# One fused attention and mixture-of-experts kernel: the packing stage's loads, score buffers and weight conversion rearranged

## Chip, cores and metric

The kernel runs on one core of one Trainium2 chip. The metric is device microseconds (us) of one execution; three runs of the kernel before gave a median of 1285.65 us (1284.27 to 1286.92). The core has five engines that run side by side and wait for one another by semaphores: TensorE (PE), VectorE (DVE), ScalarE (ACT), GpSimd (POOL) and SyncE (SP), which here issues nearly all DMAs.

## What is computed

The reference, cut to what matters (8 batches, 8 heads, 576 positions of 64; 32 packing queries; 4608 tokens of 512):

```
p_packed = sm_attn(p, k, v)              # 32 packing queries per head over 576 keys
out      = sm_attn(q, p_packed, p_packed)
x = transpose(out) to (4608, 512)
h = x @ w_in;  g = 0 below -1, (h+1)^2/4 between, h above 1;  x = g @ w_out     # d_ff 2048
expert = argmax(x @ w_gate) of 8
out[mask] = gate * (relu(x[mask] @ w1[e]) @ w2[e])                              # per expert
```

The dense weights arrive as float64 bit patterns (two 32-bit words an element) and are turned into float32 on the chip, each split into a high and a low part, since every float32 product is made of three matmuls in a shorter format (high by high, high by low, low by high).

## The kernel before

**Packing stage.** For each of 16 groups `i` (8 batches, two groups of four heads each) the kernel loads K (`kp`, 576 KB, L372) and V (`vr`, 512 and 64 KB, L376 and L377), forms the scores `sc` on PE (L385), takes their maximum on DVE (L392), exponentiates on ACT (L395), transposes the result on PE (`tp`, `av`, L403 and L405), copies it out of PSUM on ACT (L406 to L408) and multiplies it by V (`av`, L418). `build_pk` (L169) then turns the packed rows into operands (`bt`, L173, read out by ACT and DVE, L182 to L184). K and V have three places each, `kp0` to `kp2` and three for `vr`, so the loads for group i + 3 go where group i was. `sc` has one buffer of two PSUM banks (L351).

**Weights beside it.** 16 units of dense weights, 1 MB each (`wr`, L264), are converted one half at a time by `prep_half` (L267): one ACT pass (L282), four DVE passes on integers and floats (L283 to L286), a cast to the high part on ACT (L287) and the low part on DVE (L288), all 128 x 512. Units 0 and 1 of every four are first-layer weights: they go to a staging place (`ws0`, `ws1`), are multiplied by the packed operands (`first_product`, `pp`, L326; its result `pw`, L329 and L330), and are written back to DRAM by `spill` (L304) for the later batches. The other two are second-layer weights and stay (`wo`). NU = 9 units are converted in the packing loop (L459), spread evenly over its 16 turns; the other seven follow one in each of the first steps of the dense layer (L1009). The raw data of a unit shares three places (`RAW`, L254), so the load of unit u + 3 is issued behind the conversion of unit u.

**Dense layer.** 12 token tiles in 16 steps each. A step makes 128 hidden columns (`h`, `ffn1`, L698), applies the nonlinearity on ACT and DVE (`hidden`, L715 to L731), and adds the previous step's part to the output (`tile_y`, three or four PSUM banks `y`, L703 to L705). Three of the 16 steps of tile 0 are written inside the packing loop (L467). PE, ACT, DVE and POOL instructions are put in order by a list scheduler, so pieces of step 0 and later steps stand among the packing's instructions; SP keeps the order in which the program is written. Behind the dense layer come routing and the expert slots.

The PSUM has eight banks. Before, `y` has three, which `bt` and the second scores `s` (L211) share in the packing stage (L166); `h` one, `a` two, `sc` two. After packing the two banks of `sc` become `late` (L1013).

Of the kernel before, what the change touches and what calls it, by code (L numbers as in the profile page):

```python
# [8 lines left out]
F32 = mybir.dt.float32  # L9
# [28 lines left out]
NU = 9  # L38
# [53 lines left out]
def attn_moe_kernel(ctx, tc, qT, kT, vv, pT, wcat, wg, w2cat, out):  # L92
# [15 lines left out]
    wsd = dram.tile([2 * NQ, 2, P, 2, 512], F32, name="wsd")  # L108
# [12 lines left out]
    pool.memset(half, 0.5)  # L121

# [70 lines left out]
    def attn_chain(col0, b, ws, n, g, ah, al, pl, sfx):  # L193
# [73 lines left out]
    def prep_half(u, i):  # L267

        raw = wraw[u][:, i]
        n, m = divmod(u, 4)  # L270
        if m < 2:
            w = wtile(f"ws{m}{i}", [P, 2, 512], F32R, f"ws{u}_{i}")
            wstage[2 * n + m, i] = w
        else:
            if i == 0:
                wout[2 * n + m - 2] = wtile(f"wo{2 * n + m - 2}", [P, 2, 2, 512], F32R, f"wo{u}")
            w = wout[2 * n + m - 2][:, i]
        hi, lo = w[:, 0, :], w[:, 1, :]
        low, high = raw[:, :, 0], raw[:, :, 1]
        ca = s1.tile([P, 512], I32, name=f"ca{u}_{i}", tag="ca", bufs=4)  # L280
# [9 lines left out]
    loaded = [0]  # L290

    def more_units(n):
        while loaded[0] < n:
            load_unit(loaded[0])
            loaded[0] += 1

    def after_unit(u, n):
        if u and (u - 1) % 4 < 2:
            spill((u - 1) // 4, (u - 1) % 4)
        more_units(min(u + 4, n))  # L300

    def spill(n, g):
        for q in range(2):
            sp.dma_start(wsd[2 * n + g, q], f32(wstage[2 * n + g, q]))  # L304

    def reload(p, n, k):
        w = wtile(f"ws1{k % 2}", [P, 2, 512], F32R, f"ws{p}_{n}_{k}")
        sp.dma_start(f32(w), wsd[2 * n + k // 2, k % 2])
        wstage[2 * n + k // 2, k % 2] = w
# [6 lines left out]
    def first_product(n, g):  # L316
# [4 lines left out]
        for par in range(2):  # L321
            ps = a_tile([P, 512], f"pp0_{n}_{g}_{par}")
            i = 0
            for q in range(2):
                for t, m in ((0, 0), (0, 1), (1, 0)):
                    pe.matmul(ps, lhsT=one(2 * g + q, t, par), rhs=wstage[2 * n + g, q][:, m, :], start=(i == 0), stop=(i == 5))  # L326
                    i += 1
# [4 lines left out]
    def product(p, n, k):  # L332
# [5 lines left out]
        for i, (t, m) in enumerate(((0, 0), (0, 1), (1, 0))):  # L338
            pe.matmul(ps, lhsT=both(k, t), rhs=wstage[2 * n + g, q][:, m, :], start=(i == 0), stop=(i == 2))
# [756 lines left out]
```

## Time and profile before

| | us |
|---|---|
| median of three runs | 1285.65 |
| the profiled execution, its own time | 1285.13 |
| its span, first to last instruction | 1283.1 |

The profile is of that one execution. Beside the busy time of each engine it gives the share of the 16 DMA engines' time, the DMA rate, and the clock that TensorE was granted. A row of the timeline is: start, duration, engine, line, operation, result and operand, shapes, count, and in brackets how long the engine stood idle before and what released it.

### The profile page before, as it was taken

The page shows a single profiled execution, that of the slowest core. Times are in us where ns is not written, and L with a number is a line of the kernel's source. Part 1 is how long each engine was busy: PE and PEld are TensorE (multiplying, and loading weights), DVE is VectorE, ACT ScalarE, POOL GpSimd, SP SyncE. Part 2 cuts the span into 40 slices and gives each one's busy share as a digit, 9 for nine tenths or more (in the row PEclk, how much of TensorE's full clock was granted, in tenths as well). Part 3 has the DMA queues.
Part 4 walks back from the last instruction along what each step waited for, and adds up shares of the span by engine and source line. Part 5 has one row for each costly group of instructions (what it writes and reads, how often), then busy time and mean ns, then how long its engine had stood idle before and what let it go on. Part 6 is the DMA issues. An engine that isn't in the chain of part 4 may idle for free. (4 is left out here: it accounts for less than half of the span.)

```text
span 1283.1 us, 22131 instructions
## 1 busy us (share of the span) xinstructions
PE 1206.7 (94%) x7234; PEld 999.4 (78%) x7234; DVE 947.2 (74%) x2440; ACT 755.5 (59%) x1733; POOL 422.2 (33%) x682
## 2 busy tenths in 40 slices
PE   3778999999999999999999998998999999999997
PEld 2446778788778887678888876776899999999996
DVE  6766996988885959978769598688566665666653
ACT  4646666667665567566565555644556556566563
POOL 3220014723841205741112266767312112121120
PEclk9889999999999999999999999899999999999999
DMA  8967782044111232111331104201521211112150
GB/s 297 322 241 255 268 255 83 34 142 159 44 36 50 74 125 86 51 41 37 124 105 38 44 9 161 62 1 51 164 75 34 67 34 55 46 42 59 34 173 21
DMA packets 71339, 128.26 MB, mean 100 GB/s; under 512 B 10409, under 2 KB 46761, under 8 KB 69040
## 3 DMA queue, kind: packets, MB, share of 16 engines
q1 hardware_dynamic: 56528, 96.28, 22.9%
q0 software_dynamic: 5840, 18.95, 3.9%
q10 hardware_dynamic: 8848, 11.54, 2.9%
q8 instruction: 60, 0.98, 0.3%
q14 instruction: 63, 0.52, 0.1%
HBM read 162.31 MB, written 31.77 MB: 151 GB/s over the span
## 5 line engine op out<-in xcount | busy, mean ns | idle before, releaser
L698 PE MATMUL h<-ah,pw 128*128 128x256 f32 (+1 forms) x1024 | 243.1, 302 | 15.4 <-DVE rt L717 14.3
L868 PEld LDWEIGHTS gh<-gx,sw 128*128 128x128 f32 x1728 | 231.4, 193 | 14.2
L506 DVE CUSTOM_DVE_ANT_0 jk<-yr,wgb 128x512 bf16<-128x512 f32 x288 | 232.0, 806 | 9.9 <-ACT yr L756 7.9
L868 PE MATMUL gh<-gx,sw 128*128 128x256 f32 x1728 | 235.4, 285 | 0.0
L703 PE MATMUL y<-wo,gh 128*128 128x512 f32 x576 | 231.4, 402 | 2.1 <-ACT gh L730 1.2
L704 PE MATMUL y<-wo,gh 128*128 128x512 f32 x576 | 228.6, 397 | 0.0
L852 DVE TENSOR_TENSOR sw<-raw,sw 128x512 fp32r<-128x512 f32 x264 | 169.5, 693 | 74.9 <-ACT sw L851 74.9
L698 PEld LDWEIGHTS h<-ah,pw 128*128 128x128 f32 x1024 | 175.8, 189 | 40.9 <-DVE rt L717 23.3
L851 ACT CAST sw<-raw 128x512 fp32r<-128x512 f32 x304 | 169.2, 617 | 59.7 <-PE gy L705 55.4
L705 PE MATMUL y<-wo,gl 128*128 128x512 f32 x576 | 187.9, 399 | 1.6 <-POOL gl L731 1.2
L715 ACT ACTIVATE rt<-h,half 128x320 f32<-128x320 f32 (+1 forms) x192 | 111.2, 580 | 110.1 <-PE h L698 69.6
L698 PE MATMUL h<-al,pw 128*128 128x256 f32 (+1 forms) x512 | 152.4, 298 | 0.4 <-POOL al L232 0.4
L730 ACT CAST gh<-rt 128x256 fp32r<-128x256 f32 (+2 forms) x256 | 100.6, 417 | 80.1 <-DVE rt L717 57.8
L717 DVE SCALAR_TENSOR_TENSOR rt<-h,rt 128x320 f32<-128x320 f32 (+1 forms) x192 | 105.5, 550 | 51.4 <-ACT rt L716 49.7
L703 PEld LDWEIGHTS y<-wo,gh 128*128 128x128 f32 x576 | 108.8, 189 | 26.9 <-ACT gh L730 4.7
L705 PEld LDWEIGHTS y<-wo,gl 128*128 128x128 f32 x576 | 105.7, 189 | 29.0 <-POOL gl L731 2.9
L704 PEld LDWEIGHTS y<-wo,gh 128*128 128x128 f32 x576 | 109.1, 189 | 18.5
L836 POOL TENSOR_TENSOR gx<-xT,gx 128x1024 fp32r<-128x1024 f32 (+1 forms) x19 | 45.1, 2376 | 235.6 <-ACT gx L835 220.4
L704 PE MATMUL gy<-sw,ggh 128*128 128x512 f32 x288 | 115.0, 399 | 0.0
L703 PE MATMUL gy<-sw,ggh 128*128 128x512 f32 x288 | 114.7, 398 | 0.0
L872 ACT ACTIVATE ggh<-gh 128x256 fp32r<-128x256 f32 x144 | 55.0, 382 | 98.4 <-PE gh L868 93.8
L731 DVE TENSOR_TENSOR gl<-rt,gh 128x64 fp32r<-128x64 f32 (+1 forms) x192 | 92.4, 497 | 23.0 <-ACT gh L730 15.2
(221 smaller groups left out, 1874.9 us busy)
## 6 DMA issues: line engine op xcount, KB each, us to landing
raw<-in_w2cat SPq DMA_DIRECT2D x76, 1024.0 KB
ws<-wsd SPq DMA_DIRECT2D x48, 512.0 KB
wr<-in_wcat SPq DMA_DIRECT2D x16, 1024.0 KB
kp<-in_kT SPq DMA_DIRECT2D x16, 576.0 KB
xb<-xs SPq DMA_DIRECT2D x72, 128.0 KB
vr<-in_vv SPq DMA_DIRECT2D x16, 512.0 KB
wsd<-ws SPq DMA_DIRECT2D x16, 512.0 KB
qr<-in_qT ACTq DMA_DIRECT2D x16, 320.0 KB
```

Of the source, the lines that this page charges most:

```text
L506: dve.tensor_tensor_reduce(out=junk, in0=rows[j][:, :DM], in1=wgb[0][:, e, :], scale=1.0, scalar=0.0, op0=ALU.mult, op1=ALU.add, accum_out ...
L698: pe.matmul(ps[:, col0:col0 + n], lhsT=w[:, g, part, c], rhs=x[:, g, col0:col0 + n], start=(n_mm == 0), stop=(n_mm == 5))
L703: pe.matmul(y, lhsT=gh, rhs=wh, start=first, stop=False)
L704: pe.matmul(y, lhsT=gh, rhs=wl, start=False, stop=False)
L705: pe.matmul(y, lhsT=gl, rhs=wh, start=False, stop=last)
L715: act.activation(v[:, :W], ps[:, :W], AF.Relu, bias=half, scale=0.5)
L717: dve.scalar_tensor_tensor(out=v[:, :W], in0=ps[:, :W], scalar=1.0, in1=v[:, :W], op0=ALU.max, op1=ALU.min)
L730: act.copy(hi, v[:, c0:c1])
L731: lo_eng.tensor_tensor(out=lo, in0=v[:, c0:c1], in1=f32(hi), op=ALU.subtract)
L851: act.copy(w[:, 0, :], r)
L852: lo_engine(sid, i, n).tensor_tensor(out=w[:, 1, :], in0=r, in1=f32(w[:, 0, :]), op=ALU.subtract)
L868: pe.matmul(ps[:, :SL], lhsT=first(sid, 4 * (fc // 4) + k, part)[:, c], rhs=rh[:, k, :], start=(n_mm == 0), stop=(n_mm == 3 * KD - 1))
```

## The change

Groups' loads, units and PSUM banks of the packing stage are rearranged:

- K and V of a group are loaded separately: K of group i + 3 and V of group i + 2 in turn i, and each unit's load two units ahead, behind the V load. At the start, unit 0 stands between K and V of group 0, unit 1 in group 1, unit 2 behind K of group 2 (before: all three units between group 0 and group 1).
- A unit is converted whole: 128 x 1024 passes, one staging place each for `ws0` and `ws1`, one write-back DMA instead of two, sent behind the product that reads the unit. In tile 1 and later, other users of `ws0` and `ws1` (`kept`, `gx`, `reload`) take the joined places.
- NU = 12 units are converted in the packing loop, four behind it. Units 12 to 15 are loaded at the end of the loop's turn 15.
- `sc` has two buffers (four banks). Until they are given back in turn 15, only one bank `y0` serves `bt`, `s` and `y`; then four `late` banks open (`y1`, `y2`, `h`, `a2`), during the last turns instead of behind the loop.
- The loads of `qr` (queries of tile 0) during packing go from the ACT queue to SP. A one-element exponential `warm` stands at the start of ACT.

```diff
-NU = 9
+NU = 12
...
+    warm = const.tile([P, 1], F32, name="warm")
+    act.activation(warm, half, AF.Exp)
...
+    n_y = [0]
+    def y_tile(name):
+        i = n_y[0] % 3 if late else 0
+        n_y[0] = i + 1
+        return (late[0] if i else psm).tile([P, 512], F32, name=name, tag=f"y{i}")
...
-            return psm.tile([P, 512], F32, name=name, tag="y", bufs=3)
+            return y_tile(name)
...
-            act.dma_start(qr[:, :, :n], qT[b, 2 * g:2 * g + 2, :, ws:ws + n].rearrange("q p s -> p q s"))
+            (act if done else sp).dma_start(qr[:, :, :n], qT[b, 2 * g:2 * g + 2, :, ws:ws + n].rearrange("q p s -> p q s"))
...
-    def prep_half(u, i):
+    def prep_unit(u):
...
-        low, high = raw[:, :, 0], raw[:, :, 1]
-        ca = s1.tile([P, 512], I32, name=f"ca{u}_{i}", tag="ca", bufs=4)
+        low, high = raw[:, :, :, 0], raw[:, :, :, 1]
+        ca = s1.tile([P, 2, 512], I32, name=f"ca{u}", tag="ca", bufs=2)
...
     def spill(n, g):
-        for q in range(2):
-            sp.dma_start(wsd[2 * n + g, q], f32(wstage[2 * n + g, q]))
+        sp.dma_start(wsd[2 * n + g], f32(wstage[2 * n + g]))
...
-        with tc.tile_pool(name="st1p", bufs=1, space=PSUM) as p1:
+        p1_cm = tc.tile_pool(name="st1p", bufs=2, space=PSUM)
+        p1 = p1_cm.__enter__()
...
             s1_load(0)
-            more_units(3)
+            load_unit(0)
+            s1_load_v(0)
             s1_load(1)
+            load_unit(1)
+            s1_load_v(1)
             s1_load(2)
+            load_unit(2)
...
+                if i == NG - 1:
+                    p1_cm.__exit__(None, None, None)
+                    late.append(ctx.enter_context(tc.tile_pool(name="late", bufs=1, space=PSUM)))
...
                 if i + 3 < NG:
                     s1_load(i + 3)
-                for u, j in halves[2 * NU * i // 16:2 * NU * (i + 1) // 16]:
-                    prep_half(u, j)
-                    if j == 1:
-                        if u % 4 < 2:
-                            todo.append((u // 4, u % 4))
-                        after_unit(u, 12)
+                if i + 2 < NG:
+                    s1_load_v(i + 2)
+                for u in range(-(-NU * i // NG), min(-(-NU * (i + 1) // NG), NU)):
+                    prep_unit(u)
+                    if 0 < u < NU - 2:
+                        load_unit(u + 2)
+                    if u % 4 < 2:
+                        todo.append((u // 4, u % 4))
                 if i >= 5 and todo and todo[0][0] < 2:
-                    first_product(*todo.pop(0))
+                    first_product(*todo[0])
+                    spill(*todo.pop(0))
+                if i == NG - 1:
+                    for u in range(NU, FC):
+                        load_unit(u)
...
             for n, g in todo:
                 first_product(n, g)
+                spill(n, g)
```

How the change moves instructions is shown at three places. In these rows `kp0` to `kp2` are the places of K, `vr0` is V of group 0, `wr0` the raw data of unit 0, `wsd` the write-back in DRAM; a number behind an underscore only tells buffers apart.

On SP, the first loads of the program, behind the packing queries (before, then the change):

```order
L372 DMA kp0_158<-in_kT 128x2x576
L376 DMA vr0_170<-in_vv 128x4x256
L377 DMA vr0_170<-in_vv 64x256
L264 DMA wr0_175<-in_wcat 128x2048
L264 DMA wr1_177<-in_wcat 128x2048
L264 DMA wr2_179<-in_wcat 128x2048
L372 DMA kp1_160<-in_kT 128x2x576
L376 DMA vr1_184<-in_vv 128x4x256
L377 DMA vr1_184<-in_vv 64x256
L372 DMA kp2_162<-in_kT 128x2x576
L376 DMA vr2_190<-in_vv 128x4x256
L377 DMA vr2_190<-in_vv 64x256
```

```order
L371 DMA kp0_160<-in_kT 128x2x576
L275 DMA wr0_174<-in_wcat 128x2048
L379 DMA vr0_176<-in_vv 128x4x256
L380 DMA vr0_176<-in_vv 64x256
L371 DMA kp1_162<-in_kT 128x2x576
L275 DMA wr1_182<-in_wcat 128x2048
L379 DMA vr1_184<-in_vv 128x4x256
L380 DMA vr1_184<-in_vv 64x256
L371 DMA kp2_164<-in_kT 128x2x576
L275 DMA wr2_190<-in_wcat 128x2048
L439 DMA pc1_167<-in_pT 128x512
L371 DMA kp0_160<-in_kT 128x2x576
```

K of group 1 stood behind three units and now stands behind one; V of group 2 has moved behind the next group's K.

On PE, around the last scores (`sc15`), before and in the change. `h0_4` is step 4 of tile 0, `y0_2` the third output bank of tile 0; x4 counts matmuls:

```order
L698 MATMUL h0_4_1562<-ah0_194,pw0_1_1_852 128x256
L403 MATMUL tp14_1250<-ident_73,kp2_162 128x128 x4
L385 MATMUL sc15_1270<-kp0_158 64x288 x4
L405 MATMUL av13_1200<-ident_73,kp1_160 64x128
L418 MATMUL av13_1200<-vr13_993 32x64 x20
L403 MATMUL tp15_1303<-ident_73,kp0_158 128x128 x4
L405 MATMUL av14_1255<-ident_73,kp2_162 64x128
L703 MATMUL y0_3_1403<-wo2_509,gh0_1346 128x512
```

```order
L714 MATMUL h0_1_1339<-ah0_193,pw0_0_1_593 128x256
L388 MATMUL sc14_1186<-kp2_164 64x288 x4
L719 MATMUL y0_2_1362<-wo2_356,gh0_1306 128x512
L720 MATMUL y0_2_1362<-wo2_356,gh0_1306 128x512
L421 MATMUL av13_1166<-vr13_1059 32x64 x20
L388 MATMUL sc15_1238<-kp0_160 64x288 x4
L721 MATMUL y0_2_1362<-wo2_356,gl0_1307 128x512
L714 MATMUL h0_2_1383<-ah0_193,pw0_0_0_592 128x256
```

Before, `h0_1` to `h0_4` and three banks of two steps of `y` stand ahead of `sc15`; in the change `h0_1` and the first two matmuls of `y0_2` do, and `tp14` has moved behind it.

On SP, from the last K load on (before, then the change):

```order
L372 DMA kp0_158<-in_kT 128x2x576
L376 DMA vr15_1147<-in_vv 128x4x256
L377 DMA vr15_1147<-in_vv 64x256
L304 DMA wsd_72<-ws5_0_932 128x1024
L304 DMA wsd_72<-ws5_1_996 128x1024
L264 DMA wr9_1160<-in_wcat 128x2048
L264 DMA wr10_1268<-in_wcat 128x2048
L264 DMA wr11_1331<-in_wcat 128x2048
L304 DMA wsd_72<-ws8_0_1313 128x1024
L304 DMA wsd_72<-ws8_1_1322 128x1024
L264 DMA wr12_1539<-in_wcat 128x2048
```

```order
L371 DMA kp0_160<-in_kT 128x2x576
L379 DMA vr14_1114<-in_vv 128x4x256
L380 DMA vr14_1114<-in_vv 64x256
L275 DMA wr11_1126<-in_wcat 128x2048
L379 DMA vr15_1174<-in_vv 128x4x256
L380 DMA vr15_1174<-in_vv 64x256
L275 DMA wr12_1285<-in_wcat 128x2048
L275 DMA wr13_1287<-in_wcat 128x2048
L275 DMA wr14_1289<-in_wcat 128x2048
L275 DMA wr15_1291<-in_wcat 128x2048
L299 DMA wsd_72<-ws8_992 128x2048
L299 DMA wsd_72<-ws9_1117 128x2048
```

Unit 11's load moves in among the last groups' loads. Units 12 to 15 now stand directly behind the last V load, and the write-backs of units 8 and 9 (`ws8`, `ws9`) behind all four.

## Rows read from the trace of the kernel before

**Rows 1.** The page: the span, and each engine's busy time.

```profile
span 1283.1 us, 22131 instructions
...
PE 1206.7 (94%) x7234; PEld 999.4 (78%) x7234; DVE 947.2 (74%) x2440; ACT 755.5 (59%) x1733; POOL 422.2 (33%) x682
```

**Rows 2.** Busy time by stretch: length, engines, then clock, DMA share, GB/s.

```profile
0.00:122.00 122.00, 83.23 (x873) 51.38 (x875) 84.83 (x213) 66.52 (x179) 25.39 (x110) 0.93 0.80 276
122.00:136.00 14.00, 12.55 (x136) 9.31 (x137) 6.96 (x16) 8.42 (x20) 0.00 (x0) 1.00 0.97 354
136.00:186.00 50.00, 46.68 (x279) 36.41 (x277) 50.00 (x98) 33.60 (x60) 4.67 (x5) 1.00 0.71 240
...
200.00:1283.10 1083.10, 1050.25 (x5880) 890.46 (x5878) 800.26 (x2103) 640.33 (x1464) 389.01 (x564) 0.99 0.21 68
```

**Rows 3.** Who waited for whom, 0 to 122 us (total, times, longest); then SP's queue.

```profile
PE tp L403 <- ACT kp L395: 14.3, 6, 7.0
...
PE sc L385 <- DMA kp<-in_kT: 10.0, 2, 7.0
...
SPq L376 <- PE av L418: 68.5, 12, 11.2
```

**Rows 4.** SP's timeline: a stop at a V load, and the last K load.

```profile
20.91 0.54 SPq L372 DMA_DIRECT2D kp<-in_kT  x1
32.71 0.37 SPq L376 DMA_DIRECT2D vr<-in_vv  x1
...
114.64 0.58 SPq L372 DMA_DIRECT2D kp<-in_kT  x1
```

**Rows 5.** PE's timeline: scores 1, a step of h and y, and scores 15.

```profile
18.60 1.71 PE L385 MATMUL sc<-kp 128*64 128x288 f32 x6 [1.25 <-DVE ws L288]
...
104.41 0.28 PE L698 MATMUL h<-ah,pw 128*128 128x256 f32 x1
...
105.85 0.39 PE L703 MATMUL y<-wo,gh 128*128 128x512 f32 x1
106.08 0.40 PE L704 MATMUL y<-wo,gh 128*128 128x512 f32 x1
...
121.91 0.95 PE L385 MATMUL sc<-kp 128*64 128x288 f32 x6
```

**Rows 6.** The page's list of DMA issues: count and size of each kind.

```profile
wr<-in_wcat SPq DMA_DIRECT2D x16, 1024.0 KB
kp<-in_kT SPq DMA_DIRECT2D x16, 576.0 KB
...
vr<-in_vv SPq DMA_DIRECT2D x16, 512.0 KB
wsd<-ws SPq DMA_DIRECT2D x16, 512.0 KB
```

**Rows 7.** Busy time in the two stretches in which loads ran without a gap.

```profile
8.00:24.00 16.00, 6.82 (x63) 3.31 (x59) 12.14 (x28) 10.12 (x22) 4.44 (x10) 1.00 1.04 369
40.00:64.00 24.00, 17.30 (x192) 9.74 (x190) 20.51 (x55) 15.54 (x52) 6.16 (x14) 0.86 1.00 357
```

**Rows 8.** DVE's timeline: passes of 128 x 512, one directly behind the other.

```profile
142.02 0.42 DVE L284 TENSOR_SCALAR ca<-ca 128x512 int32<-128x512 int32 x1
142.35 0.68 DVE L286 SCALAR_TENSOR_TENSOR ca<-wr,ca 128x512 int32<-128x512 int32 x1
142.95 0.69 DVE L731 TENSOR_TENSOR gl<-rt,gh 128x512 fp32r<-128x512 f32 x1
```

**Rows 9.** DVE groups by shape: the same operation at 512 and at 256 columns.

```profile
L731 DVE TENSOR_TENSOR gl<-rt,gh 128x512 fp32r<-128x512 f32 x64 | 45.3, 708 | 12.2 <-ACT gh L730 10.9 <-PE pp L339 0.7 <-ACT ah L231 0.3
...
L731 DVE TENSOR_TENSOR gl<-rt,gh 128x256 fp32r<-128x256 f32 x64 | 27.6, 431 | 0.4
```

**Rows 10.** PE and ACT timelines: the first `bt` and the last copy that reads it.

```profile
16.65 0.48 PE L173 MATMUL bt<-ident,packed 128*64 128x128 f32 x2 [0.71 <-ACT packed L419]
...
28.38 0.18 ACT L184 COPY pkf<-bt 64x32 f32<-64x32 f32 x1
```

More of the change, by code (lines that the diff above doesn't have):

```diff
@@ L288, in prep_half @@
         dve.tensor_tensor(out=lo, in0=f32(ca), in1=f32(hi), op=ALU.subtract)
[L290 to L300, printed above, removed]
     def spill(n, g):
-        for q in range(2):
-            sp.dma_start(wsd[2 * n + g, q], f32(wstage[2 * n + g, q]))
+        sp.dma_start(wsd[2 * n + g], f32(wstage[2 * n + g]))
+    ws1 = [None]
     def reload(p, n, k):
-        w = wtile(f"ws1{k % 2}", [P, 2, 512], F32R, f"ws{p}_{n}_{k}")
-        sp.dma_start(f32(w), wsd[2 * n + k // 2, k % 2])
-        wstage[2 * n + k // 2, k % 2] = w
+        if n == k == 0:
+            ws1[0] = wtile("ws1", [P, 2, 2, 512], F32R, f"ws_{p}")
+        sp.dma_start(f32(ws1[0][:, k % 2]), wsd[2 * n + k // 2, :, k % 2])
     def products(p, n):
@@ L325, in first_product @@
                 for t, m in ((0, 0), (0, 1), (1, 0)):
-                    pe.matmul(ps, lhsT=one(2 * g + q, t, par), rhs=wstage[2 * n + g, q][:, m, :], start=(i == 0), stop=(i == 5))
+                    pe.matmul(ps, lhsT=one(2 * g + q, t, par), rhs=wstage[2 * n + g][:, q, m, :], start=(i == 0), stop=(i == 5))
                     i += 1
@@ L338, in product @@
         for i, (t, m) in enumerate(((0, 0), (0, 1), (1, 0))):
-            pe.matmul(ps, lhsT=both(k, t), rhs=wstage[2 * n + g, q][:, m, :], start=(i == 0), stop=(i == 2))
+            pe.matmul(ps, lhsT=both(k, t), rhs=ws1[0][:, q, m, :], start=(i == 0), stop=(i == 2))
         for par in range(2):
@@ L722, in hidden @@
             if fc == 0:
-                kept[:] = [wtile(f"ws0{i}", [P, FC, HB], F32R, f"kept{t}_{i}") for i in range(2)]
+                kt = wtile("ws0", [P, 2, FC, HB], F32R, f"kept{t}")
+                kept[:] = [kt[:, i] for i in range(2)]
             parts = [(0, SPLIT, gh[:, :SPLIT], gl[:, :SPLIT]), (SPLIT, W, kept[0][:, fc], kept[1][:, fc])]
@@ L737, in tile_y @@
         if fc == 0:
-            y_tiles[t] = [psm.tile([P, 512], F32, name=f"y{t}_{j}", tag="y", bufs=3) for j in range(min(3, len(gs)))]
+            y_tiles[t] = [y_tile(f"y{t}_{j}") for j in range(min(3, len(gs)))]
             if len(gs) > 3:
@@ L831, in slot_x @@
         n_x[0] += 1
-        xh, xl = (wtile(f"ws{n_x[0] % 2}{i}", [P, KD, SL], F32R, f"gx{sid}_{i}") for i in range(2))
+        gx = wtile(f"ws{n_x[0] % 2}", [P, 2, KD, SL], F32R, f"gx{sid}")
+        xh, xl = gx[:, 0], gx[:, 1]
         for k in range(KD):
@@ L879, in slot_y @@
         if fc == 0:
-            sl["y"] = [psm.tile([P, 512], F32, name=f"gy{sid}_{tb}", tag="y", bufs=3) for tb in range(2)]
+            sl["y"] = [y_tile(f"gy{sid}_{tb}") for tb in range(2)]
         ffn2(second(sid, fc, 0), second(sid, fc, 1), sl["g"][fc], sl["y"], fc == 0, fc == FC2 - 1)
```

30 lines of the change are left out of this document (14 added, 16 removed).

## The prediction
> **What bounds the kernel now.** I read the page first: PE is busy for 1206.7 of 1283.1 us [rows 1], so 76.4 us of idle time are all that another order can win, beside matmuls that ran slowly (the granted clock was 0.93 before 122 us [rows 2]). The table of stretches tells where they lie [rows 2]: 38.8 us before 122 us, where the packing stage is, 1.4 and 3.3 us in the next two, and 32.9 us spread over the last 1083 us. At 122 us PE begins the scores of the last group [rows 5]; from there it is all but full. So the question is when the last scores start, and how much PE has done by then.
>
> In those 122 us no engine is full: PE 68%, DVE 84.83 us or 70%, the DMA engines 80% at 276 GB/s [rows 2]. The list of waits shows a chain instead [rows 3]: PE stands 14.3 us for the exponential and 10.0 us for K. Only one of K's waits is long, that at the very start; but SP's own queue stood 68.5 us in twelve waits for `av`, each ahead of a V load. SP's timeline shows one: K of group 4 at 20.91, then nothing until V of group 4 at 32.71 [rows 4]. All loads behind it wait too. Where loads run without a gap, the engines move 369 and 357 GB/s, and DVE works for 20.51 of 24 us [rows 7]. The stage could run like that throughout; it does for 40 of 122 us.
>
> **The start.** K, V, a unit and half a write-back have their sizes in the list of DMAs [rows 6], the others follow from their shapes (a packing-query load and a `qr` of tile 0 are 0.26 MB, V 0.59 MB in two pieces, K 0.59, a unit 1.05). Ahead of and with K of group 1 stand 0.26 + 2 x 0.59 + 3 x 1.05 + 0.59 = 5.2 MB before. At 369 GB/s, from about 2 us on, that is 16 us; its scores start at 18.60 [rows 5]. In the change it is 0.26 + 2 x 0.59 + 1.05 + 0.59 = 3.1 MB, or 10.4 us. The head start is some 6 to 10 us at the second group, since what then queued behind three units' conversion comes earlier too. `warm` takes the load of the exponential's table off the first group, about 1 us, and is inside this.
>
> **The pace.** When can the last scores start? Two floors and a choice.
> - Loads: ahead of and with K of group 15 SP now issues 16 K, 14 V, 11 units, 4 whole write-backs, 4 `qr` and 2 packing loads: 9.44 + 8.26 + 11.53 + 4.19 + 1.05 + 0.52 = 35.0 MB. At 369 GB/s and 2 us to start: 97 us. (Before: 33.1 MB on all queues, K issued at 114.64 [rows 4].)
> - DVE: nine units were converted by then, now eleven. Back to back, a 128 x 512 pass of two operands takes 0.60 us start to start (142.35 to 142.95), one of a single operand 0.33 (142.02 to 142.35) [rows 8]. A unit was 2 x (3 x 0.60 + 2 x 0.33) = 4.92 us. 256 columns more cost 0.28 us (708 against 431 ns) [rows 9], 512 then 0.55, half of it for a single operand: a whole pass is 1.15 or 0.60 us, and a unit 4.65. So 51.2 instead of 44.3 us, +7; one step of h less, with its two passes, -1.2: 84.8 + 5.8 = 90.6 us. Some 2 us of these lie in the first 8, when nothing has arrived: 8 + 88.6 = 97 us too.
> - At the DVE share of the dense stretch, 20.51 of 24 us or 85% [rows 7], 88.6 us take 104: the last maximum is at 112, its scores start a matmul group earlier, at **110 us**. This I take: both floors are at 97, but in-order engines that hand work round will not reach them. Ends: 97, and 122 if nothing is gained.
>
> So 121.9 - 110 = 11.9 us earlier.
>
> **What is owed.** PE has done less by then. Before, four more steps of `h` than step 0 stand ahead of `sc15`, and 18 matmuls of `y`; now one step and two matmuls. A step is 1.44 us (104.41 to 105.85), a `y` matmul 0.23 (105.85 to 106.08) [rows 5]: 3 x 1.44 + 16 x 0.23 = 8.0 us. Against it `av13` is done and `tp14` not: about -0.5. **7.5 us** of PE work are pushed behind the last scores, where PE is full, and count in full. Hence break-even: the last scores at 114.4 us.
>
> **Behind the packing.** Before, DVE was busy for all 50 us from 136 to 186 [rows 2], with seven units, and PE lost 3.3 us there. Now five units fall behind the last scores and DVE has slack. Late next are loads: units 12 to 15 wait for `tp15`, 14 us of PE work behind `sc15`, and the write-backs of units 8 and 9 follow behind them: 5 x 1.05 MB at 354 GB/s [rows 2] is 15 us, so unit 8's place is free some 31 us after `sc15` starts. The cast of unit 12 into it stands on ACT amid step 6 of `h`, whose first `y` matmul PE reaches after 41 us; the cast and the three passes behind it take 4. I count 4.5 us idle in place of the 4.8 before: **-0.3**, between -4 and +5.
>
> **Small edits.** A second score buffer lets PE run ahead, but PE's waits for the exponential were in front of `tp`, not of `sc`: alone, 0 to -3 us; in the pace. `qr` leaves ACT (four issues of 0.4 us) for SP, behind other loads; the last stands at 28.8 MB, 80 us at full rate, and is wanted behind the scores of group 11, some 85 us in at the pace above: 0, up to +3. One write-back DMA instead of two: in the pace. The joined `ws` places later hold the same bytes in the same order: 0, with 1 us either way.
>
> **Sum.** 1285.13 - 11.9 + 7.5 - 0.3 = 1280.4. The median of the runs is 0.5 above that execution: **1281.0 us**, 0.4% faster. A measurement can tell about 0.2%, 2.6 us, from no change.
>
> **A rule against the count.** The timeline shows 0.60 us between starts where each pass itself lasts 0.68 [rows 8], so when DVE is full, joining two passes saves under 0.1 us. The Trainium skill (VectorE: DVE Perf Modes, section "The TRN2 errata") says that every instruction pays a fixed latency, and gives (N + 151)/0.96 ns for a float32 operation of two tensors: two of 512 would cost 1.38 us, one of 1024 1.22. By that rule a unit would save 0.8 us rather than 0.25, and eleven 6 us; the trace agrees with it on one pass alone (0.68 us) but not on a full queue.
>
> **Rivals.**
> 1. *The fixed part counts.* DVE seldom has two passes ready at once while packing, so 0.68 each is the price, and joining saves 0.13 (0.68 - 0.55) on each of five pairs in eleven units, 7 us instead of 2.8. Then 84.4 us at 85%: 105 for the scores, 1276. The trace has idle gaps between passes (DVE 70%), which speaks for it; the full 24 us speak against. 0.08.
> 2. *Full pace.* With SP no longer held by V the loads stay queued and the rest keeps up: scores at 100 to 101, 1271 to 1272. For: the 369 GB/s. Against: DVE would be at 95%. 0.12.
> 3. *One bank instead of three.* `bt`, `s` and the first `y` share `y0`. The first `bt` is written at 16.65 and last read at 28.38 [rows 10], 12 us or two groups; the next waits in PE's order ahead of `av` and scores. Eight users, some three caught for 1.5 us each: 4.5 us, scores at 114.5, **1285.5**, no difference. 0.22.
> 4. *Slower: the pace of the loads does not rise.* The queue is freer, but carries 1.9 MB more ahead of the last K, and the casts of units 4 and 5 into the single `ws0` and `ws1` wait on ACT for write-backs that stand at 19.5 and 22.7 MB in SP's order, ahead of the exponentials. If that keeps the mean near 276 to 300 GB/s, K arrives between 119 and 129 us. At 300: scores at 119, 1285.1 - 2.9 + 7.5 - 0.3 + 0.5 = **1290**. It decides from below 310 GB/s. For: 38.8 us of idle came from such crossings, and DVE's passes are now twice as long in front of each maximum. Against: the stretch at 357 GB/s held write-backs too. 0.18.
>
> My forecast, scores between 106 and 113, has 0.40: 1277 to 1284, mostly over 0.2% faster. **Chances**: faster 0.40 x 0.95 + 0.08 + 0.12 = 0.58 and a bit of case 3: 0.60. Same: 0.22. Slower: 0.18. The **range** of 1270 to 1290 takes in cases 2 and 3 and the milder half of 4; the forecast's own is 1277 to 1284.
>
> **What would show it.** Right: the last scores near 110 us; DVE at 80% or more and the DMA share near 0.9 until then; SP's waits for `av` well under 68.5 us; two or three units' worth of full DVE gone behind the packing; idle PE time before the last scores down by 8 to 12 us, and the same 33 us later on. Wrong: the last scores after 114; PE waiting for `bt` or `s` on `y0`; ACT standing at a cast into `ws0` or `ws1` for a DMA, with an exponential behind it; PE idle over 6 us in the 80 us after the last scores.

## The result and the profile after

Beside runs of the kernel before at 1286.29 us (1284.27 to 1287.01), the changed kernel took **1273.28 us** (1272.29 to 1274.38, four runs each): a ratio of 0.9904, 95% interval 0.989 to 0.9918. I had forecast 1281.0, range 1270 to 1290. The direction was right, the size was not: 4.7 us were forecast, 13.0 came. The profiled execution took 1273.13 us, its span is 11.7 us shorter.

The page's first lines for the changed kernel, as [rows 1]: PE is busy for 1.0 us less, so 10.7 of the 11.7 us are idle time.

```profile
span 1271.4 us, 21999 instructions
...
PE 1205.7 (95%) x7234; PEld 999.5 (79%) x7234; DVE 943.2 (74%) x2360; ACT 752.5 (59%) x1702; POOL 420.8 (33%) x682
```

Its table of stretches, as [rows 2] (length, busy time of PE, weight loads, DVE, ACT and POOL, then clock, DMA share, GB/s):

```profile
0.00:122.00 122.00, 89.88 (x947) 54.19 (x948) 97.00 (x187) 73.28 (x176) 26.37 (x110) 0.86 0.88 312
122.00:136.00 14.00, 14.00 (x118) 11.25 (x116) 6.22 (x9) 8.52 (x15) 0.00 (x0) 1.00 0.62 242
136.00:186.00 50.00, 50.00 (x269) 41.48 (x268) 38.23 (x60) 28.01 (x45) 7.20 (x8) 1.00 0.80 261
...
200.00:1271.40 1071.40, 1037.83 (x5833) 880.39 (x5831) 795.08 (x2093) 633.31 (x1447) 383.27 (x556) 0.99 0.22 68
```

PE's idle time fell from 38.8 to 32.1 us before 122 us and from 4.8 to nothing from there to 200 us. Fixed times hide that the work has shifted, so I divide both traces where the work agrees: at the last scores (121.91 before, 111.43 now), at the first copy of an output bank of tile 0 (206.08 and 196.25; up to there PE has done the same matmuls in both, but for a handful), and at the first of the four copies that end tile 4 (487.22 and 476.06). The same view of the kernel before:

```profile
0.00:121.91 121.91, 83.14 (x871) 51.29 (x871) 84.83 (x213) 66.52 (x179) 25.39 (x110) 0.93 0.80 276
121.91:206.08 84.17, 79.40 (x516) 62.44 (x516) 65.55 (x131) 52.03 (x99) 9.97 (x12) 1.00 0.74 253
206.08:487.22 281.14, 277.58 (x1430) 225.10 (x1429) 226.40 (x659) 182.38 (x472) 113.94 (x216) 1.00 0.23 78
```

and of the changed kernel:

```profile
0.00:111.43 111.43, 79.88 (x857) 46.59 (x857) 87.60 (x171) 65.79 (x160) 26.37 (x110) 0.85 0.96 341
111.43:196.25 84.82, 84.26 (x532) 69.21 (x527) 57.51 (x91) 49.68 (x88) 9.29 (x14) 1.00 0.59 198
196.25:476.06 279.81, 277.32 (x1434) 225.08 (x1433) 227.61 (x661) 182.47 (x473) 111.35 (x215) 1.00 0.24 79
```

| stretch | before | after | difference |
|---|---|---|---|
| to the last scores | 121.91 | 111.43 | -10.5 |
| to the end of tile 0: PE busy | 79.40 | 84.26 | +4.9 |
| the same: PE idle | 4.77 | 0.56 | -4.2 |
| tiles 1 to 4 | 281.14 | 279.81 | -1.3 |
| the rest | 795.88 | 795.34 | -0.5 |

Together -11.7. The granted clock worked against the change: up to the last scores it was 0.85 on average over the half and the full speed that the trace shows, and 0.93 before. PE's busy time for its 7234 matmuls isn't the same in all kernels of this text either: it goes from 1196.9 us (c_nu8) to 1206.7 (the kernel before). So a difference between two runs need not be all idle time.

The waits of the changed kernel before the last scores, as [rows 3]: for PE, then SP's own queue.

```profile
PE tp L406 <- ACT kp L398: 11.8, 6, 3.1
PE sc L388 <- DMA kp<-in_kT: 6.4, 1, 6.4
...
SPq L275 <- PE tp L406: 22.2, 1, 22.2
SPq L379 <- PE av L421: 16.0, 5, 4.4
SPq L212 <- POOL al L243: 10.4, 1, 10.4
```

SP stood 68.5 us for `av` before and 16.0 now. The 22.2 us are the load of unit 12 behind the last V and hold nothing up. New is the last row: SP's timeline shows the write-back at 52.00, then nothing until the third `qr` load, with K right behind it.

```profile
52.00 0.38 SPq L299 DMA_DIRECT2D wsd<-ws  x1
64.99 0.38 SPq L212 DMA_DIRECT2D qr<-in_qT  x1
65.42 0.46 SPq L371 DMA_DIRECT2D kp<-in_kT  x1
```

`qr` has two places; the third load waits until the first chain has read its place out. By the DMA share this is the only gap in the load stream:

```profile
8.00:64.00 56.00, 40.95 (x477) 23.30 (x474) 45.62 (x94) 36.27 (x100) 9.61 (x28) 0.89 1.04 372
64.00:72.00 8.00, 7.40 (x30) 4.70 (x28) 6.18 (x12) 3.90 (x8) 2.79 (x5) 0.71 0.71 219
72.00:104.00 32.00, 23.63 (x279) 13.26 (x279) 26.93 (x48) 18.67 (x40) 7.10 (x12) 0.79 1.05 375
```

### The profile page after: what moved, and what is told of

It reads as the page before. It is cut to its first block, busy times and chain, and to the rows that moved or that the text cites. A ratio compares the mean times of both kernels' runs of the same rounds, so it can differ in the third digit from the quotient of the medians.

```text
span 1271.4 us, 21999 instructions
## 1 busy us (share of the span) xinstructions
PE 1205.7 (95%) x7234; PEld 999.5 (79%) x7234; DVE 943.2 (74%) x2360; ACT 752.5 (59%) x1702; POOL 420.8 (33%) x682
## 5 line engine op out<-in xcount | busy, mean ns | idle before, releaser
L721 PE MATMUL y<-wo,gl 128*128 128x512 f32 x576 | 191.8, 399 | 2.4 <-POOL gl L748 2.0
L720 PEld LDWEIGHTS y<-wo,gh 128*128 128x128 f32 x576 | 108.9, 189 | 18.4
```

The lines of the kernel that those rows point to most:

```text
L720: pe.matmul(y, lhsT=gh, rhs=wl, start=False, stop=False)
L721: pe.matmul(y, lhsT=gl, rhs=wh, start=False, stop=last)
```

## The experiments

Each run stood beside runs of the kernel before on the same chip. "End of tile 0" is the first copy of an output bank; it compares kernels that have done different work by the last scores. One caution for all: the list scheduler places many rows elsewhere for any edit, so a difference of a few us in one run may be order alone. The runs are of five batches; the median of the kernel before lay between 1285.2 and 1287.3 us in them. Where the intervals of two ratios overlap widely, the difference of the two medians is not shown to be one; the text says so at each such place.

| run | median, us | ratio (95% interval) | last scores | PE busy by then | end of tile 0 |
|---|---|---|---|---|---|
| the change | 1273.3 | 0.9904 (0.989 to 0.9918) | 111.4 | 79.9 | 196.3 |
| a_vk | 1278.5 | 0.9936 (0.9916 to 0.9956) | 113.7 | 80.2 | 199.1 |
| a_sc1 | 1280.8 | 0.9958 (0.9942 to 0.9974) | 115.6 | 79.6 | 200.3 |
| a_nu9 | 1275.8 | 0.9911 (0.9883 to 0.9939) | 113.0 | 79.3 | 199.2 |
| a_qr_act | 1271.6 | 0.988 (0.9854 to 0.9907) | 109.3 | 77.7 | 194.4 |
| a_skip | 1288.3 | 1.0033 (1.0018 to 1.0048) | 121.0 | 77.2 | 210.4 |
| a_lo_pool | 1280.7 | 0.9966 (0.9954 to 0.9978) | 113.7 | 75.5 | 203.0 |
| a_half | 1272.0 | 0.9902 (0.9877 to 0.9926) | 112.0 | 77.7 | 196.8 |
| a_uf | 1282.7 | 0.998 (0.9967 to 0.9993) | 116.7 | 76.0 | 202.7 |
| a_skip_qr | 1278.9 | 0.9956 (0.9933 to 0.9979) | 107.3 | 69.9 | 200.2 |
| a_nu9_qr | 1265.6 | 0.9841 (0.9824 to 0.9857) | 98.6 | 70.4 | 188.0 |
| a_nu10_qr | 1272.2 | 0.9889 (0.9872 to 0.9905) | 105.1 | 72.1 | 194.2 |
| b_order | 1274.1 | 0.9903 (0.9887 to 0.992) | 111.5 | 80.2 | 196.2 |
| c_load2 | 1278.8 | 0.993 (0.9913 to 0.9946) | 116.3 | 80.0 | 200.9 |
| c_dve2 | 1269.5 | 0.9863 (0.9846 to 0.9879) | 101.9 | 71.7 | 192.9 |
| c_sc1 | 1268.6 | 0.985 (0.9834 to 0.9866) | 108.4 | 81.7 | 189.9 |
| c_nu8 | 1265.0 | 0.9827 (0.9807 to 0.9846) | 100.3 | 70.3 | 187.9 |
| c_dram | 1270.9 | 0.9886 (0.9865 to 0.9907) | 108.9 | 78.1 | 192.4 |
| c_half | 1266.3 | 0.9847 (0.9828 to 0.9867) | 102.0 | 70.8 | 187.8 |

### One part of the change undone

**The V loads (a_vk).**

```diff
                     s1_load(i + 3)
-                if i + 2 < NG:
-                    s1_load_v(i + 2)
+                    s1_load_v(i + 3)
```

> The changed kernel with one part undone: V of group i + 3 is loaded with K of group i + 3 again (V of group 2 with K of group 2 at the start). Theory 1 (the loads' order is the gain: SP stood 68.5 us at V loads before, 16.0 us in the changed kernel): SP stands for av again, 50 us or more in total before 110 us, the last scores start at 117 to 122 us in place of 111.4, the run is at 1278 to 1284 us. Rival (the second score buffer and the whole-unit passes carry the gain, the queue's stops were idle time of no consequence): last scores within 2 us of 111.4, 1272 to 1275 us.

SP's queue stood for `av` again:

```profile
SPq L379 <- PE av L421: 56.4, 12, 8.3
```

The last scores came only 2.3 us later, the run was 5.2 us slower (its profiled execution, 1275.92 us, was the fastest of five). So SP's long waits need not be a loss: while SP stood, the loads already issued kept the DMA engines busy here (share 0.98 until the last scores, against 0.80 in the kernel before). The sum of a queue's waits was a poor measure.

**The start (a_uf).**

```diff
-            load_unit(0)
             s1_load_v(0)
+            for u in range(3):
+                load_unit(u)
             s1_load(1)
-            load_unit(1)
             s1_load_v(1)
             s1_load(2)
-            load_unit(2)
```

> The changed kernel with the start order of before: K and V of group 0, three units, then K and V of group 1, then K of group 2. My count was 6 to 10 us for this at the second group (scores 1 at 13.0 us in the changed kernel, 18.6 before). If that head start lasts, the last scores come 5 us or more later, run at 1277 to 1282 us. Theory 4 (the same bytes stand ahead of the last K in either order, so the load stream ends at the same time): second scores at 18 to 19 us, but the last within 2 us of 111.4, run at 1272 to 1276 us.

The second scores start at 16.95 in place of 13.02, the last 5.2 us later, and the run is 9.4 us slower. The head start lasts. Equal bytes ahead of the last K do not make the two orders equal: the DMA share until the last scores is 0.91 in place of 0.96, and SP stood 49.5 us for `av`. That the later start is what stalls the queue further on is likely, not shown.

**The PSUM part (a_sc1):** one score buffer, three `y` banks, late banks behind the loop.

```diff
+        return psm.tile([P, 512], F32, name=name, tag="y", bufs=3)
...
-        p1_cm = tc.tile_pool(name="st1p", bufs=2, space=PSUM)
+        p1_cm = tc.tile_pool(name="st1p", bufs=1, space=PSUM)
```

> The changed kernel with the PSUM part undone: one score buffer of two banks, three banks of y from the start, the late banks opened behind the packing loop. Theory 1 (the loads carry the gain): the last scores start within 2 us of 111.4 us, the whole run at 1272 to 1276 us; more h steps stand ahead of the last scores again. Rival (the second buffer lets PE run ahead of the maximum and the exponential, and the four late banks keep PE fed behind the packing): last scores at 115 us or later, or PE idle by 3 us or more in the 80 us behind them, 1278 to 1284 us.

It lost 7.5 us: 4.2 at the last scores, 2.5 in PE's idle time up to the end of tile 0 (3.11 against 0.56 us), and 3.4 behind it, where it took 1078.5 against 1075.1 us; PE's busy time up to the end of tile 0 gave back 2.7. Of the 3.11 us, 2.1 are one wait of `tp` for the last exponential. This was the rival's case.

**The units (a_nu9):** nine beside the packing; the loads of the later ones are moved to fit.

```diff
-NU = 12
+NU = 9
```

> The changed kernel with 9 units converted beside the packing, as before, and seven in the first dense steps (raw data loaded two units ahead, the last four at the end of the loop and behind unit 11). Theory 2 (PE's 4.2 us of idle time that vanished behind the packing went because DVE has two or three units less to convert there): DVE is full again for 40 us or more in the 50 us behind the packing, PE idles there 3 to 8 us, while the last scores come 3 to 7 us earlier than 111.4 since DVE has three units less to convert by then; the sum is 1272 to 1278 us. Rival (the idle time went for another reason, the four late banks that open in the last turns): PE idle below 1 us in the 80 us behind the last scores with nine units too, and the run is at or below 1272 us.

Both sides missed. The last scores came 1.6 us *later* although DVE had finished eight units by then and not ten (78.0 us busy, not 87.6), and PE idled for only 1.2 us behind them although DVE had eight units left there and was busy for 48.0 of the 50 us from 127 us on. Waits for DVE make up 1.0 of the 1.2 us. So the units explain at most a part of the idle time that vanished behind the packing. The run's 2.5 us more are not shown (0.9911 against 0.9904). The late scores go with SP's stop: it stood 19.5 us at the third `qr` load, first for `s`, then for `al`.

```profile
SPq L212 <- POOL al L243: 13.3, 1, 13.3
SPq L379 <- PE av L421: 11.6, 3, 5.9
SPq L212 <- PE s L222: 6.2, 1, 6.2
```

**Halves (a_half):** all five DVE passes 128 x 512 again.

> The changed kernel with each unit converted in two halves of 512 columns again, everything else as in it. My count: joining two passes saves 0.25 us a unit, nothing to be seen. Rival 1 of the prediction (0.13 us on each of five pairs in eleven units, 7 us of DVE): last scores 3 to 6 us later than 111.4, run at 1276 to 1279 us. Theory 4 (loads set the pace, DVE has room): last scores within 2 us, run at 1272 to 1275 us; shorter passes in front of each maximum may even help by 1 us.

No difference. DVE was busy for 89.7 us before the last scores in place of 87.6: joining the passes of the ten to eleven units by then saved some 2.1 us, against the 2.8 of my count. By single durations it would be much: the five pairs of a unit take 2 x (0.435 + 0.440 + 0.706 + 0.687 + 0.69) = 5.92 us in this trace, five whole passes 5.13 in the changed kernel. That 0.79 us is what the Trainium skill's rule gives (VectorE: DVE Perf Modes, "The TRN2 errata"); DVE's busy time shows a quarter of it, since passes in a queue overlap [rows 8], and nothing of it reached the end.

**`qr` back on ACT's queue (a_qr_act).**

```diff
-            (act if done else sp).dma_start(qr[:, :, :n], ...)
+            act.dma_start(qr[:, :, :n], ...)
```

> The changed kernel with the qr loads of tile 0 issued by ACT again. In the changed kernel SP stood from 52.0 to 65.0 us at the third of them, with every later load behind it, and the DMA share fell to 0.71 in the 8 us behind. Theory 3 (that stop costs time on the path to the last scores): the stop is gone, the last scores start 3 to 8 us earlier than 111.4, 1267 to 1271 us. Rival (loads are far enough ahead that the stop is made good by the faster stretch behind it, and ACT pays for its four issues): last scores within 1.5 us of 111.4, 1272 to 1275 us.

The stop is gone and the last scores come 2.1 us earlier: between the two theories. The run takes 1.7 us less, which is not shown to be a gain (0.988 against 0.9904, the intervals overlap). The DMA share now stayed at 1.03 or more from 8 to 96 us.

### What sets the pace

**Loads left out (a_skip, a_skip_qr),** with `qr` on SP and on ACT:

```diff
+        if u in (3, 5, 7, 9):
+            wraw[u] = kept_raw[u - 3]
+            return
...
+        wraw[u] = kept_raw[u] = raw
```

> The changed kernel with four of the twelve unit loads beside the packing left out: units 3, 5, 7 and 9 convert the raw data of the unit three before them once more (so part of the weights are other numbers; every engine's work is as before). It takes 4.2 MB out of the load stream and nothing else. In the changed kernel the DMA engines were full from 8 to 104 us but for one stop. Theory 4 (the load stream is what now sets the last scores): 4.2 MB at some 370 GB/s are 11 us; last scores at 100 to 104 us in place of 111.4, run at 1265 to 1270 us. Rival (DVE's passes set the pace, as I had counted it): last scores within 2 us of 111.4, run at 1272 to 1275 us.

> The changed kernel with the qr loads on ACT's queue and, again, units 3, 5, 7 and 9 not loaded (they convert the raw data of the unit three before them, so part of the weights are other numbers). In the first run without these loads SP stood 27.5 us at the third and fourth qr load, and nothing of the load stream could be read from it. With the qr loads on ACT alone the DMA engines were full from 8 to 102 us and the last scores at 109.3. Theory 4 (the load stream sets the last scores where nothing stops SP): 4.2 MB or 11 us less of it, last scores at 97 to 101 us. Rival (the chain scores, maximum, exponential, transpose, av sets the pace, and the full DMA engines are only kept busy by what is queued): last scores at 107 to 110 us.

Both missed. In the first, SP stood at the third `qr` load from 50.0 to 77.4 us, 13.5 us for `s` and then 14.0 for `al` (both waits are of this one load, not of two as the second expectation says). No K was issued between 44.87 and 77.83 us, and the kernel became slower than before with less to load. In the second the last scores came 2.0 us earlier than in a_qr_act, where 8 to 12 were expected, PE had done 7.8 us less by then, and the run was some 7 us slower. SP stood 53.8 us for `av` in it, so groups came slower than loads. What held them, the twelve conversions or the order of the rows, these two runs do not tell.

**DVE relieved by POOL (a_lo_pool).**

```diff
-        dve.tensor_tensor(out=lo, in0=f32(ca), in1=f32(hi), op=ALU.subtract)
+        pool.tensor_tensor(out=lo, in0=f32(ca), in1=f32(hi), op=ALU.subtract)
```

> The changed kernel with the low part of every unit (the last of its five DVE passes, 1.23 us each) made by POOL instead, whose busy time before the last scores was 26 of 111 us. DVE has some 13 us less to do until the last scores. Rival of theory 4 (DVE sets the pace at 85% of its time): last scores at 97 to 102 us, run at 1266 to 1270 us. Theory 4 (the load stream sets it): last scores within 3 us of 111.4, since not a byte less is moved, or later where POOL's slower pass delays units; run at 1271 to 1277 us.

Slower by 7.4 us. The run does not tell the theories apart, since DVE got slower too (see the last section).

**Nine or ten units, `qr` on ACT (a_nu9_qr, a_nu10_qr).**

> The changed kernel with the qr loads on ACT's queue and 9 units beside the packing in place of 12. With 9 units and the qr loads on SP the last scores came 1.6 us later, not earlier, SP having stood 19.5 us at the qr loads. Theory 4: two units fewer stand ahead of the last K, 2.1 MB or 6 us: last scores at 102 to 105 us in place of 109.3; behind them PE idles some 1 to 3 us and has more work left, run at 1269 to 1273 us. Rival (units beside the packing cost it nothing, since the chain sets the pace): last scores at 107 to 111 us, run at 1272 to 1276 us.

> The changed kernel with the qr loads on ACT's queue and 10 units beside the packing. Theory 4: one to two units fewer ahead of the last K, 3 to 6 us: last scores at 103 to 107 us in place of 109.3, run at 1268 to 1272 us. Rival (the chain sets the pace): last scores at 107 to 111 us, 1271 to 1274 us.

With nine units the last scores start at 98.6 and the run takes 1265.6 us, 7.7 less than the change and 0.6% faster. With ten they come 4.2 us earlier than with twelve, but the run gains nothing (1272.2 against 1271.6): PE idles for 3.4 us behind them. The two parts work against each other: taking three units from the packing gained 5.9 us with `qr` on ACT, and nothing that can be told with it on SP. Of the 6.7 us between the profiled executions of a_qr_act and a_nu9_qr, 3.1 are idle time of PE; 3.7 are busy time (1204.5 and 1200.8 us) for the same number of matmuls. The clock until the last scores was 0.84 in the one and 0.95 in the other. Stretches of a_nu9_qr, to the last scores, to the end of tile 0 and behind:

```profile
0.00:98.58 98.58, 70.36 (x803) 41.12 (x803) 74.91 (x158) 58.17 (x151) 28.50 (x110) 0.95 1.01 358
98.58:188.01 89.43, 87.99 (x581) 71.83 (x581) 70.04 (x104) 55.83 (x96) 9.68 (x13) 1.00 0.66 218
188.01:1263.60 1075.59, 1042.46 (x5853) 884.37 (x5851) 798.35 (x2099) 636.95 (x1456) 384.77 (x560) 0.99 0.22 68
```

The DMA engines are full on average from the start to the last scores (share 1.01).

**Eight units (c_nu8).**

> The changed kernel with qr on ACT's queue and 8 units beside the packing, eight behind it. If fewer units go on gaining: last scores 4 us or more earlier than 98.6, run at 1260 to 1264 us. If DVE behind the packing is the limit by now (70.8 of 91 us busy there with nine): PE idles 4 us or more behind the last scores, run at 1265 to 1270 us.

1265.0 us: no more to be had there, within what can be told.

**More bytes, more DVE work, on a_nu9_qr.** First three units loaded twice into one place (c_load2), then the same bytes copied from DRAM to DRAM (c_dram), then one DVE pass of every unit done twice (c_dve2):

```diff
-        sp.dma_start(raw.rearrange("p h a b -> p (h a b)"), wcat[u])
+        for _ in range(2 if u in (3, 5, 7) else 1):
+            sp.dma_start(raw.rearrange("p h a b -> p (h a b)"), wcat[u])
```

```diff
+        if u in (3, 5, 7):
+            sp.dma_start(wsd[u // 2 + 4].rearrange("p a b c -> p (a b c)").bitcast(I32), wcat[u])
```

```diff
-        dve.tensor_tensor(out=lo, in0=f32(ca), in1=f32(hi), op=ALU.subtract)
+        for _ in range(2 if u < NU else 1):
+            dve.tensor_tensor(out=lo, in0=f32(ca), in1=f32(hi), op=ALU.subtract)
```

> The changed kernel with qr on ACT's queue and 9 units beside the packing (last scores 98.6 us, run at 1265.6), and units 3, 5 and 7 each loaded twice in a row into the same place: 3.1 MB more in the load stream, no other work. Theory 4 (the load stream sets the pace; the DMA share was 1.01 until the last scores): 3.1 MB at some 375 GB/s are 8 us, last scores at 105 to 108 us, run at 1270 to 1275 us. Rival (DVE sets it, at 76% of its time as in the other runs): last scores at 97 to 101 us, run at 1264 to 1268 us.

> The changed kernel with qr on ACT's queue and 9 units beside the packing (last scores 98.6 us, run at 1265.6), and behind the loads of units 3, 5 and 7 a copy of the same 1 MB from DRAM to a part of the write-back area that is not in use yet: 3.1 MB more in the stream on the same queue, nobody waits for it. Theory 4 (bytes set the pace): last scores at 105 to 108 us, run at 1270 to 1275 us. Rival (stops of SP, not bytes, made the run with doubled loads slow): last scores at 97 to 102 us, run at 1264 to 1269 us.

> The changed kernel with qr on ACT's queue and 9 units beside the packing, and the last DVE pass of each of those units done twice: 9 x 1.23 = 11 us more on DVE, not a byte more. Theory 4 (the load stream sets the pace): last scores at 97 to 101 us in place of 98.6, run at 1264 to 1268 us. Rival (DVE sets it; at 76% of its time 11 us become 14): last scores at 109 to 113 us, run at 1272 to 1278 us. In between, 102 to 108 us: both are near their limits and each adds a part.

c_load2 was spoilt by its own edit, since the second copy had to wait for the first and SP with it:

```profile
SPq L276 <- DMA wr<-in_wcat: 31.0, 6, 10.0
```

c_dram has no such wait. Its rows to the last scores and to the end of tile 0, then the same of c_dve2:

```profile
0.00:108.87 108.87, 78.14 (x873) 46.33 (x873) 78.51 (x163) 62.54 (x160) 25.48 (x110) 0.87 1.01 363
108.87:192.38 83.51, 82.00 (x511) 67.46 (x511) 66.20 (x99) 51.84 (x88) 10.22 (x13) 1.00 0.68 221
```

```profile
0.00:101.86 101.86, 71.69 (x802) 41.98 (x803) 83.81 (x166) 56.36 (x150) 29.30 (x110) 0.89 0.98 344
101.86:192.92 91.06, 87.98 (x581) 71.91 (x581) 70.68 (x105) 57.50 (x97) 10.41 (x13) 0.99 0.64 218
```

8 us more of stream put the last scores back by 10.3 us, but PE had done more by then: 24 `h`, 6 `y` and 40 `av` matmuls. At the end of tile 0, where the work agrees, 4.4 us are left; the run takes 5.2 us more. c_dve2 has the same matmuls ahead of the last scores as a_nu9_qr. 11 us more of DVE, some 9 of them by then, put them back by 3.3 us, the end of tile 0 by 4.9, and the run by 3.9. So both hold the kernel up in part, the stream by a half to two thirds of what is added and DVE by a third to a half. These two runs do not tell which is the nearer limit, and c_dram's lower clock until the last scores (0.87 against 0.95) is in its figure. c_load2, with the same bytes as c_dram and the stops, lost 13.2 us: SP's stops cost about as much as the bytes, or more.

### One part alone, and a ladder

**The loads' order on the kernel before (b_order).**

```diff
+            more_units(1)
+            s1_load_v(0)
+            s1_load(1)
+            more_units(2)
+            s1_load_v(1)
+            s1_load(2)
             more_units(3)
-            s1_load(1)
-            s1_load(2)
...
                     s1_load(i + 3)
+                if i + 2 < NG:
+                    s1_load_v(i + 2)
```

> The kernel before with the loads' order of the change alone: the start with unit 0 behind K of group 0 and unit 1 behind K of group 1, V loaded two groups ahead, behind the K load three groups ahead. One score buffer, halves, 9 units, qr on ACT as before. Theory 1 (order of the loads carries the gain by itself): last scores at 111 to 114 us in place of 121.9, run at 1275 to 1279 us. Rival (order and second score buffer need each other: with one buffer PE waits for the exponential wherever the loads stand; the run with one buffer in the changed kernel lost 7.5 us): last scores at 116 to 120 us, run at 1280 to 1285 us.

1274.1 us, ratio 0.9903: **the order of the loads alone gives what the whole change gives**, with one score buffer, halves and nine units. Both halves of the order have a share: in the changed kernel, the old start cost 9.4 us (a_uf) and the old place of the V loads 5.2 (a_vk).

```profile
0.00:111.52 111.52, 80.22 (x860) 49.71 (x860) 84.01 (x213) 66.32 (x179) 27.03 (x110) 0.88 0.89 311
111.52:196.23 84.71, 81.33 (x532) 64.31 (x532) 68.94 (x138) 53.63 (x108) 11.86 (x17) 1.00 0.72 242
```

**The fastest kernel without the PSUM part (c_sc1), and with halves (c_half).**

> The changed kernel with qr on ACT's queue and 9 units beside the packing, and with the PSUM part undone: one score buffer, three banks of y from the start, the late banks behind the loop. If the PSUM part is worth by itself what it cost to take it from the changed kernel (7.5 us): last scores at 102 to 105 us in place of 98.6, PE idle by 3 us behind them, run at 1271 to 1275 us, close to the kernel before with the new order of loads alone (1274.1). Rival (with fewer units and no stop of SP, the exponential is early enough for one buffer): last scores within 2 us, run at 1265 to 1269 us.

> The changed kernel with qr on ACT's queue and 9 units beside the packing, and each unit converted in two halves of 512 columns. In the changed kernel itself halves were worth nothing (1272.0 against 1273.3 us). If whole units have no share here either: 1264 to 1268 us. If the joined passes matter where the loads no longer stop (nine units x 0.65 us of fixed part on DVE, 6 us, a third of which reached the end when a pass was doubled): last scores at 100 to 102 us, 1267 to 1270 us.

c_sc1 is slower by 3.0 us, which is not shown to be a loss (0.985 against 0.9841). Its last scores come 9.8 us later, but PE had 81.7 us of work behind it by then, not 70.4. In the profiled executions, 4.3 us apart, PE idles equally long, 62.9 and 62.8 us; they differ in its busy time (c_sc1, then a_nu9_qr), and the clock until the last scores was 0.89 and 0.95.

```profile
PE 1204.9 (95%) x7234; PEld 999.9 (79%) x7234; DVE 949.6 (75%) x2360; ACT 751.4 (59%) x1702; POOL 429.1 (34%) x682
PE 1200.8 (95%) x7234; PEld 997.3 (79%) x7234; DVE 943.3 (75%) x2360; ACT 750.9 (59%) x1702; POOL 423.0 (33%) x682
```

c_half shows again that whole passes have no share.

These make a ladder, each step one part more (medians): before 1286.3; loads' order 1274.1; whole units with their loads, places and write-backs, and `warm`, 1268.6 (c_sc1); PSUM part 1265.6 (a_nu9_qr); twelve units 1271.6 (a_qr_act); `qr` on SP 1273.3 (the change). The steps are -12.2, -5.5, -3.0, +5.9 and +1.7 us. The ratios are 0.9903, 0.985, 0.9841, 0.988 and 0.9904: the first, second and fourth step are clear of the noise or nearly so, the third and the fifth are not. So twelve units gave back about what whole units with their loads had gained. What of the second step is due to which of its parts (not to the passes, by c_half) wasn't tried.

## Why the prediction was wrong in size

The sum was -11.9 + 7.5 - 0.3 = -4.7. The trace has -10.5 + 4.9 - 4.2 - 1.9 = -11.7.

- **The start: right in kind, a little short.** Scores 1 at 13.02 in place of 18.60, 5.6 us, forecast 6 to 10; undone, it cost 5.2 us at the last scores.
- **The pace: the number right, its reason only in part.** The last scores start at 111.43, forecast 110. I took DVE at 85% of its time as the limit; it was busy for 87.6 of 111.4 us, 79%. With two units less by then the scores were no earlier (a_nu9), with 9 us more only 3.3 later (c_dve2). The stream and its stops counted too: c_dram, c_load2, and the 13 us stop at `qr`. And b_order reaches the same 111.5 us with none of the other parts: the gain that I had spread over loads, score buffer and passes is the loads' order by itself. PE's idle time by then fell by 7.2 us, just under the 8 to 12 that I had named as a sign. I also left the clock out of the sum; it was 0.85 until then and not 0.93.
- **What is owed: nearly right by count.** Ahead of the last scores 36 `h` and 16 `y` matmuls fewer are done, 8.0 us as forecast. From there to the end of tile 0 there are in turn 40 `av` and four `s` fewer and four `tp` more, by their rows some 0.9, 0.8 and 0.6 us, for which I had allowed half a us: 6.9 owed in place of 7.5. But PE's busy time there grew by only 4.9. The other 2.0 us I read as gaps that busy time hides: an `h` matmul counts 0.28 us when it stands alone and 0.12 in a row [rows 5], and before, more stood alone.
- **Behind the packing: the step that failed.** I wrote "4.5 us idle in place of the 4.8". PE idled for 0.56 us, so the term was -4.2 and not -0.3, or -6.2 with those 2.0 us. The cast of unit 12 that I saw coming stood where I put it: it starts at 143.57 us, 32 us behind the last scores (counted: 31). But PE waited for nothing there; it had other work in its order. I had set a new wait in place of the old ones without asking what else PE could do at that moment. The longest old wait, 2.5 us for DVE, is gone too. It lay where DVE was busy for all of 136 to 186 us [rows 2]; in the change DVE is busy for 38.2 of the same 50. PE's longest waits behind the last scores, before and in the change:

```profile
168.22 0.39 PE L698 MATMUL h<-ah,pw 128*128 128x256 f32 x1 [2.48 <-DVE rt L717]
```

```profile
PE y L719 <- ACT kp L398: 0.6, 1, 0.6
```

Which part of the change removed the old waits stays open. Nine units alone bring back 0.7 us (a_nu9 idles 1.2), the PSUM part undone 2.5 (a_sc1). But with nine units and no PSUM part c_sc1 idles 1.1 us, and a_nu10_qr, with the PSUM part and ten units, 3.4. The four late banks were not tried by themselves.
- **"The joined `ws` places later: 0": not shown to have failed.** From the end of tile 0 on the change takes 1.9 us less, but PE's idle time there is the same 33 us, as forecast: 32.9 before, 33.6 now. What is shorter is its busy time, 1044.2 and 1041.6 us, for the same matmuls but four:

```profile
206.08:1283.10 1077.02, 1044.17 (x5849) 885.70 (x5847) 796.86 (x2097) 636.90 (x1455) 386.84 (x561) 0.99 0.21 68
196.25:1271.40 1075.15, 1041.58 (x5853) 883.75 (x5851) 798.11 (x2099) 637.06 (x1456) 385.12 (x560) 0.99 0.22 68
```

Between 780 and 930 us the clock was 0.94 before and 0.97 now, so this is likely the clock, which the sum had left out. The sixteen kernels with the PSUM part take 1074.4 to 1076.8 us there and the four without it 1077.0 to 1078.5; that the banks save time later is not shown by this.
- **`qr` on SP, 0 to +3: inside** with twelve units (+1.7, not clear of the noise), but 10.2 us with nine (1275.8 against 1265.6). I had looked at when the data would be wanted, not at when its place would be free.
- **Rivals.** The fixed part of a pass: refuted (a_half, c_half). Full pace: its time nearly came (1271 to 1272 us), but not its scores at 100 to 101 us; with nine or eight units and `qr` on ACT they come then, at 98.6 and 100.3 (a_nu9_qr, c_nu8). One bank instead of three: PE's waits for `bt` and `s` on the one bank come to 2.3 us, not 4.5. Slower loads: 341 GB/s until the last scores, above the 310 from which that case decided.

By busy and idle time the error adds up as 3.9 (behind the packing) + 2.6 (owed) + 1.9 (later) - 1.4 (pace) = 7.0 us; by count, 5.9 of it lie behind the packing and 0.6 in what is owed.

## What to carry to other kernels

On a queue that is kept in program order, ask of every load when its *place* comes free, and what stands behind it: one load with a late place held all others for 13 us. A sum of a queue's waits tells little by itself; look also for gaps in the DMA share. Before a wait is put into a sum, look what else the engine has in its order at that moment. Before a difference of a few us is explained by waits, compare the busy time and the clock of the two runs. A change of several parts deserves its parts one by one on the kernel before: here one part had the whole gain, and undoing two of the others made one of the two fastest kernels, 1265.6 us.

## What the runs showed of the hardware

Some DVE passes were held up by POOL's. With the low part on POOL (a_lo_pool), POOL takes 2.4 us for what DVE does in 1.23, and a DVE pass of one operand that usually takes 0.68 us lasts until about 0.56 us after POOL's has ended:

```profile
77.97 2.44 POOL L296 TENSOR_TENSOR wo<-ca,wo 128x1024 fp32r<-128x1024 f32 x1
...
79.24 1.73 DVE L291 TENSOR_SCALAR ca<-ca 128x1024 f32<-128x1024 f32 x1 [2.13 <-ACT ca L290]
```

POOL ends at 80.41, DVE at 80.97. Until the last scores five passes of L291 started while POOL was at such a pass, and all five ended 0.55 or 0.56 us after it. A reduction, L395 at 86.63, overlapped the next POOL pass (86.90, 2.39 us) and took its usual 0.74 us. So some 13 us taken from DVE until the last scores made it only 5.5 us less busy (82.1 against 87.6). The Trainium skill says so of a DVE instruction that needs the port pair which the two engines share, as this kind may (SBUF — State Buffer, "Who interferes with whom"): the one that issues first holds the pair for its whole instruction, and the other waits. These rows agree.
